# The down-projection of a gated unit turned round: output columns on the partitions, the gate kept in bf16 and transposed by DMA

## The chip, the cores and the metric

The kernel runs on one core of a Trainium2 chip. The metric is device time in microseconds. Before the change the median of three runs is 803.18 us (802.27 to 803.32). Short names: PE is TensorE, ACT is ScalarE, DVE is VectorE, POOL is GpSimd, SP is SyncE, which here only issues DMAs.

## The reference

Two sub-layers read the same normalised input, and one gates the other. S is 2048 tokens, D is 640, F is 1728, with 32 heads of 20 columns.

```python
x = A_x
xn = _layernorm(x, axis=-1)
s = _A_ref(xn, A_wqkv, A_wo)              # softmax attention, then @ wo
g = _silu(_B_ref(xn, B_w_gate, B_w_up, B_w_down))
return x + s * g
# _B_ref: h = sigmoid(x @ w_gate) * (x @ w_up); return h @ w_down
```

## The kernel before

**Stages.** A first stage, written out as a list of steps, normalises the tokens, transposes them into `xnT` (columns on the partitions, four chunks of 512 tokens) and makes the first keys, values and queries. Then comes one long stage in which everything else is interleaved, and a short tail for the last attention block and the last 512 tokens of the output.

**Attention.** Eight groups of four heads times four query chunks of 512 make 32 blocks. A score tile is 128 keys by 512 queries of one head. Its exponential is made either by ACT (two tiles at once, `pt`, or one, `px`) or by DVE with integer operations (`iv`, then three passes into `pb`, four tiles at once). PE adds the tiles times the values into `oacc`. After a block, DVE copies `oacc` to `on` (line 959), the row sums go to DRAM and back in another layout (`ld`, `lt`), DVE takes reciprocals (`rt`, line 969), these go to DRAM and come back spread out (`rd`, `rl`), and POOL multiplies (`on_bf`).

**The gated unit.** For each chunk c of 512 tokens there are 14 tiles kf of 128 hidden columns. `mk_gu` makes one of them: gate and up matmuls, tanh on ACT, and a multiply on DVE (line 690) that writes `hT[:, kf, :]`, with hidden columns on the partitions and tokens along the row. `mk_down(c, t4, h)` is the second matmul for 128 tokens (t4 of 4) and half of the output columns (h of 2, 320 columns). `hT` is the stationary operand and `wd` moves, 14 steps of four matmuls that lie side by side in the array (`cols`, line 471), each 32 columns of the stationary operand. ACT makes tanh (`td`), and DVE makes (td + 1) * ps in f32 (line 740), which is stored to `gq_dram` with tokens as rows (line 742). For the last chunk DVE writes it straight into SBUF (`gq_last`, line 736).

**The output.** `mk_out(tt, h)` multiplies the attention output by `wo` for token tile tt. `load_out(tt)` has loaded x (line 770) and the gate (line 771) into one of three buffers (tt modulo 3), and DVE multiplies the sum with the gate (line 795, `otmp`). POOL adds x, and the tile is stored. The last four token tiles are done in the tail (`t_main`, `t_rest`).

**What sets the order.** The orders of PE, ACT, DVE and POOL are written out at build time by a planner (the loop at line 1229). It steps a clock of its own with the durations of lines 444 to 448, and at each step gives a free engine its next instruction. PE chooses between score matmuls, value matmuls and an item (`Item`), which holds one of three shared PSUM banks from its first matmul until its last operation marked "free". A down item books 14 steps of 0.14 us on PE, 0.32 on ACT and 0.40 on DVE. Items of the gated unit come from `glu_items`, in order, as long as the work done is at most LEAD us ahead of what is due. M_ORD, DORD and XORD say in which order the three banks are tried for an item, for a DVE score tile and for an extra ACT score tile. The order on SP is not written out: the framework places DMAs by their own readiness, and SP works them in that order.

```python
    def cols(out, lhsT, rhs, start, stop):
        for j in range(0, P, 32):
            nc.tensor.matmul(out[j:j + 32, :], lhsT=lhsT[:, j:j + 32], rhs=rhs, start=start, stop=stop,
                             tile_position=(0, j), skip_group_check=True)
```

Of the kernel before, what the change touches and what calls it, by code (L numbers as in the profile page):

```python
# [18 lines left out]
P = 128  # L19
# [32 lines left out]
def kernel(  # L52
# [394 lines left out]
    LATE, T_LT, T_OU, T_L2, T_RL = 1.0, 9.0, 1.5, 4.5, 5.6  # L447
    T_PASS = (0.1333, 0.1333, 0.27)

    def t_exp(n):  # L450
# [213 lines left out]
    def mk_gu(c, kf, at):  # L664
# [18 lines left out]
            cols(st[key], w[:, i, kd, ko * P:ko * P + P], xnT[:, c, kd, :], kd == 0, kd == KD - 1)  # L683

        def th():
            st["t"] = w2.tile([P, QC], BF16, tag="tnh", bufs=2, name="tnh")
            act_imm(st["t"][0:fs, :], st["g"][0:fs, :], ACT.Tanh, 0.5)

        def ev():
# [4 lines left out]
            cols(st["g"], wgu_tiles[(c, k2)][:, 0, kd, P:2 * P], xnT[:, c, kd, :], kd == 0, kd == KD - 1)  # L694

        def th2():
            st["t"] = w2.tile([P, QC], BF16, tag="tnh", bufs=2, name="tnh")
            act_imm(st["t"][fs:P, :], st["g"][0:fs, :], ACT.Tanh, 0.5)

        def ev2():  # L700
# [9 lines left out]

    gq_l = []

    def gq_last(t4):
        if len(gq_l) == t4 // 2:
            w = w2.tile([P, 2, KD, 2 * P], BF16, tag="wgu", bufs=2, name="gql")
            gq_l.append(w.rearrange("p i k f -> p (i k f)").bitcast(FP32))
        return gq_l[t4 // 2][:, t4 % 2 * D:(t4 % 2 + 1) * D]

    def mk_down(c, t4, h, at):
        st = {}  # L720
        tt = 4 * c + t4
# [24 lines left out]


    FL, FG, FK = (NG - 1) * GC, (NG - 2) * GC, (KD - 1) * P
# [15 lines left out]
    def load_out(tt):  # L764
        if tt in out_tiles:
            return
        o2 = xfl[:, tt % 3 * KD * QC:tt % 3 * KD * QC + 3 * D]
        flush("o")
        out_tiles[tt] = (o2[:, 0:D], o2[:, D:3 * D].bitcast(FP32))
        nc.sync.dma_start(out=out_tiles[tt][0], in_=x2[tt * P:(tt + 1) * P, :])  # L770
        nc.sync.dma_start(out=out_tiles[tt][1], in_=gq_dram[tt * P:(tt + 1) * P, :])

    def mk_out(tt, h, at):
        st = {}

        def alloc():
            if h == 0:
                load_out(tt)
                if (tt + 1) % 4:
                    load_out(tt + 1)  # L780
            st["ps"] = misc_ps()

        def mm(kd):
            hs = slice(h * HD, (h + 1) * HD)
            cols(st["ps"][:, 0:HD], oU[:, kd, tt * P:(tt + 1) * P], wo[:, kd, hs], kd == 0, kd == KD - 1)

        def ev():
            xr, gqr = out_tiles[tt]
            sl = slice(h * HD, (h + 1) * HD)
            while sum(x[1] == "o" for x in pool_q) > 2:  # L790
                x = next(x for x in pool_q if x[1] == "o")
                pool_q.remove(x)
                x[2]()
            tmp = w2.tile([P, HD], FP32, tag="gqs", bufs=3, name="otmp")
            ins = nc.vector.scalar_tensor_tensor(out=tmp, in0=st["ps"][:, 0:HD], scalar=0.25,
                                                 in1=gqr[:, sl], op0=ALU.mult, op1=ALU.mult)
# [10 lines left out]
        return Item([("PE", alloc, [(0.136, lambda kd=kd: mm(kd)) for kd in range(KD)]),  # L807
                     ("DVE", 0.40, ev, "free", mark("o", tt, h))], at, need=ALT + 1 + 2 * (tt // 4),
                    pre=[("d", tt // 4, t4, i) for t4 in range(4) for i in range(2)] + [("h", 2, kf) for kf in range(NFT)] + (
                        [("o", tt - 2, 1)] if h == 0 and tt > 1 else []))  # L810


# [1 line left out]
    for c in range(NQC):  # L814
        for kf in range(NFT):
            glu.append(lambda at, c=c, kf=kf: mk_gu(c, kf, at))
        for h in range(2):
            for t4 in range(4):
                glu.append(lambda at, c=c, t4=t4, h=h: [mk_down(c, t4, h, at)])
# [273 lines left out]
    xg = xl.rearrange("p (t u) -> p t u", u=D)  # L1093

    def t_main(t4):
        nc.vector.scalar_tensor_tensor(out=tmps[t4], in0=mains[t4], scalar=0.25, in1=gq_last(t4)[:, 0:512],
                                       op0=ALU.mult, op1=ALU.mult)
        if t4 < 2:
            nc.gpsimd.tensor_tensor(out=tail[t4][:, 0:512], in0=tmps[t4], in1=tail[t4][:, 0:512], op=ALU.add)

    def t_rest(i):
        nc.vector.scalar_tensor_tensor(out=tmp[:, 2 * i:2 * i + 2, :],
                                       in0=rest[i][:, 0:2 * EX].rearrange("p (t e) -> p t e", e=EX),
                                       scalar=0.25, in1=gq_l[i].rearrange("p (t u) -> p t u", u=D)[:, :, 512:D],
                                       op0=ALU.mult, op1=ALU.mult)
        (nc.vector if i else nc.gpsimd).tensor_tensor(out=xg[:, 2 * i:2 * i + 2, 512:D], in0=tmp[:, 2 * i:2 * i + 2, :],
                                                      in1=xg[:, 2 * i:2 * i + 2, 512:D], op=ALU.add)
# [420 lines left out]
```

## Time and profile before

| | |
|---|---|
| median of three runs | 803.18 us |
| the profiled execution | 803.98 us |
| its span, first to last instruction | 802.3 us |
| granted TensorE clock | 1.00 |
| down matmuls (`bk<-wd,hT`, 320 columns) | 1792, mean 302 ns |
| gate and up matmuls (`bk<-xnT,wgu`, 512 columns) | 2160, mean 383 ns |
| tanh of a down item (`td`, 128x320) | 32, mean 617 ns |
| tanh of a gate item (`tnh`, 128x512) | 52, mean 790 ns |
| multiply of a down item (`gqs`, `gql`) | 32, median 480 to 482 ns |
| gate loads (`xnT<-gq_dram`, 320 KB) | 12 |
| gate stores (`gq_dram<-gqs`, 160 KB) | 24 |

A line of the timeline gives the start, the time from the first start to the last end of the merged instructions, the engine, the line of the kernel, the operation, and the tiles as output<-input. The duration of one instruction includes its way through the engine, and the next one starts before it ends, so the pace of an engine is read between starts. Line 82 is the helper that issues tanh and exp on ACT, and line 473 is the matmul in `cols`, for all items that use it; the tiles tell them apart. "SPq" is the time that SP takes to issue a DMA, not that of the transfer.

### The profile page before, as it was taken

The page shows a single profiled execution, that of the slowest core. Times are in us where ns is not written, and L with a number is a line of the kernel's source. Part 1 is how long each engine was busy: PE and PEld are TensorE (multiplying, and loading weights), DVE is VectorE, ACT ScalarE, POOL GpSimd, SP SyncE. Part 2 cuts the span into 40 slices and gives each one's busy share as a digit, 9 for nine tenths or more (in the row PEclk, how much of TensorE's full clock was granted, in tenths as well). Part 3 has the DMA queues.
Part 4 walks back from the last instruction along what each step waited for, and adds up shares of the span by engine and source line. Part 5 has one row for each costly group of instructions (what it writes and reads, how often), then busy time and mean ns, then how long its engine had stood idle before and what let it go on. Part 6 is the DMA issues. An engine that isn't in the chain of part 4 may idle for free.

```text
span 802.3 us, 25398 instructions
## 1 busy us (share of the span) xinstructions
PE 780.6 (97%) x10466; PEld 285.1 (36%) x10466; DVE 769.5 (96%) x1239; ACT 781.6 (97%) x991; POOL 106.2 (13%) x219
## 2 busy tenths in 40 slices
PE   8899999999999999999999999999999999999997
PEld 5523333333433323334332332333333233333333
DVE  7799999999999999989999999999999999999996
ACT  8799999999999999999999999999999999999994
POOL 7200000000000000000000010000000100502325
PEclk9999999999999999999999999999999999999999
DMA  5441212223122223222113133222311332330421
GB/s 162 133 130 49 69 40 75 63 66 81 47 63 66 73 72 100 52 57 71 49 47 94 53 86 76 76 79 58 98 37 61 91 89 53 106 103 23 141 62 62
DMA packets 91851, 60.47 MB, mean 75 GB/s; under 512 B 34891, under 2 KB 85627, under 8 KB 91735
## 3 DMA queue, kind: packets, MB, share of 16 engines
q1 hardware_dynamic: 91447, 58.52, 26.1%
q8 instruction: 82, 1.34, 0.7%
q14 instruction: 34, 0.28, 0.1%
q10 hardware_dynamic: 288, 0.33, 0.1%
HBM read 45.18 MB, written 11.09 MB: 70 GB/s over the span
## 4 chain that ended last, share of the span: by engine, by line
PE 48%; ACT 39%; DVE 6%; issue 5%; DMA 1%; SPq 0%; POOL 0%; DVEq 0%; ACTq 0%; POOLq 0%
ACT pt L82 31%; PE bk L473 20%; PE scA L889 15%; PE oacc L926 10%; ACT px L82 4%; ACT tnh L82 2%; DVE iv L1325 2%; DVE pb L1025 1%; PE bk L889 1%; ACT td L82 1%; PE tp L292 1%; DVE pb L1022 0%; DMA xt<-in_A_x_dram 0%; PE scrap L398 0%; PE psk L142 0%
## 5 line engine op out<-in xcount | busy, mean ns | idle before, releaser
L82 ACT ACTIVATE pt<-scA 128x1024 bf16<-128x1024 f32 (+1 forms) x709 | 708.8, 1189 | 1.0 <-PE scA L889 0.4
L1325 DVE TENSOR_SCALAR iv<-bk 128x512 int16<-128x512 f32 x500 | 332.9, 684 | 12.0 <-PE bk L889 9.6
L889 PE MATMUL scA<-q,kT 32*128 32x512 bf16 x1412 | 275.9, 382 | 8.7 <-ACT pt L82 3.3
L889 PE MATMUL bk<-q,kT 32*128 32x512 bf16 x636 | 207.4, 383 | 0.0
L889 PEld LDWEIGHTS <-kT 32*128 32x128 bf16 x2048 | 88.5, 91 | 262.0 <-issue 250.6
L926 PE MATMUL oacc<-pt,v 128*21 128x512 bf16 x1412 | 178.7, 381 | 0.7 <-ACT pt L82 0.7
L926 PE MATMUL oacc<-pb,v 128*21 128x512 bf16 x1000 | 161.4, 382 | 0.0
L473 PE MATMUL bk<-xnT,wgu 128*32 128x512 bf16 x2160 | 157.3, 383 | 0.5 <-DVE iv L1325 0.2
L1025 DVE TENSOR_TENSOR pb<-iv,pb 128x2048 bf16<-128x2048 bf16 x125 | 152.5, 1220 | 0.7
L979 POOL TENSOR_TENSOR on_bf<-on,rl 128x128 bf16<-128x128 f32 x116 | 54.4, 472 | 627.3 <-DVE iv L1325 170.4
L82 ACT ACTIVATE px<-bk 128x512 bf16<-128x512 f32 x136 | 101.4, 763 | 1.7 <-POOL hT L1167 1.6
L1019 DVE TENSOR_SCALAR pb<-iv 128x2048 int16<-128x2048 int16 x125 | 87.1, 697 | 0.4
L473 PE MATMUL bk<-wd,hT 128*32 128x320 bf16 x1792 | 87.0, 302 | 0.3 <-DVE iv L1325 0.2
L1022 DVE TENSOR_SCALAR pb<-iv 128x2048 int16<-128x2048 int16 x125 | 86.7, 693 | 0.0
L926 PEld LDWEIGHTS <-v 128*21 128x21 bf16 x2548 | 53.9, 91 | 76.0 <-issue 53.5
L473 PEld LDWEIGHTS <-wgu 128*32 128x32 bf16 x2160 | 44.4, 95 | 64.3 <-issue 45.9
L473 PEld LDWEIGHTS <-hT 128*32 128x32 bf16 x1792 | 37.5, 95 | 38.5 <-issue 32.9
L473 PE MATMUL bk<-xnT,wu 128*32 128x512 bf16 x640 | 48.5, 384 | 0.6 <-DVE iv L1325 0.2
L926 PE MATMUL oacc<-px,v 128*21 128x512 bf16 x136 | 46.7, 381 | 0.0
L82 ACT ACTIVATE tnh<-bk 128x512 bf16<-128x512 f32 (+1 forms) x56 | 43.4, 776 | 0.1
L690 DVE SCALAR_TENSOR_TENSOR hT<-tnh,bk 128x512 bf16<-128x512 bf16 x52 | 35.4, 681 | 1.0 <-PE bk L889 0.3
L800 POOL TENSOR_TENSOR xnT<-otmp,xnT 128x160 bf16<-128x160 f32 x48 | 28.2, 607 | 40.4 <-PE bk L889 15.9
(119 smaller groups left out, 413.6 us busy)
## 6 DMA issues: line engine op xcount, KB each, us to landing
rl<-rd SPq DMA_DIRECT2D x124, 64.0 KB
wgu<-in_B_w_gate_dram SPq DMA_DIRECT2D x24, 320.0 KB
wgu<-in_B_w_up_dram SPq DMA_DIRECT2D x24, 320.0 KB
gq_dram<-gqs SPq DMA_DIRECT2D x24, 160.0 KB
xnT<-gq_dram SPq DMA_DIRECT2D x12, 320.0 KB
xt<-in_A_x_dram SPq DMA_DIRECT2D x16, 160.0 KB
xnT<-in_A_x_dram SPq DMA_DIRECT2D x16, 160.0 KB
out_dram<-xnT SPq DMA_DIRECT2D x14, 160.0 KB
```

Of the source, the lines that this page charges most:

```text
L82: return nc.scalar.add_instruction(mybir.InstActivation(func=func, name=nc.get_next_instruction_name(), engine=ENG.Activation, ins=[nc.sca ...
L292: nc.tensor.transpose(out=tps[k][:, kd, :], in_=xns[k][:, kd * P:(kd + 1) * P], identity=ident)
L473: nc.tensor.matmul(out[j:j + 32, :], lhsT=lhsT[:, j:j + 32], rhs=rhs, start=start, stop=stop, tile_position=(0, j), skip_group_check=True)
L690: return nc.vector.scalar_tensor_tensor(out=hT[0:fs, kf, :], in0=st["t"][0:fs, :], scalar=1.0, in1=st["u"][0:fs, :], op0=ALU.add, op1=ALU. ...
L800: add = nc.gpsimd.tensor_tensor(out=xr[:, cs], in0=tmp[:, i * HD // 2:(i + 1) * HD // 2], in1=xr[:, cs], op=ALU.add)
L889: nc.tensor.matmul(dst, lhsT=kTs[gc_of(b)[0] % 2][32 * j:32 * j + 32, kt * P:(kt + 1) * P], rhs=qts[b % 3][32 * j:32 * j + 32, :], start=T ...
L926: nc.tensor.matmul(oacc[32 * j:32 * j + DH + 1, :], lhsT=lhsT, rhs=u["src"], start=first, stop=last, tile_position=(0, 32 * j), skip_group ...
L979: ins = nc.gpsimd.tensor_tensor(out=on_bf[:, cs], in0=on[:, cs], in1=rl[:, cs], op=ALU.mult)
L1019: ins = nc.vector.tensor_scalar(out=pb[:, 0, :, :].bitcast(I16), in0=iv, scalar1=0x7F80, scalar2=1, op0=ALU.bitwise_and, op1=ALU.bitwise_or)
L1022: ins = nc.vector.tensor_scalar(out=pb[:, 1, :, :].bitcast(I16), in0=iv, scalar1=0x007F, scalar2=0x3F00, op0=ALU.bitwise_and, op1=ALU.bitw ...
L1025: ins = nc.vector.tensor_tensor(out=pb[:, 1, :, :], in0=iv.bitcast(BF16), in1=pb[:, 1, :, :], op=ALU.mult)
L1325: beat(nc.vector.tensor_scalar(out=d["iv"][:, j, :], in0=bank[bk], scalar1=B_OFF, scalar2=0.0, op0=ALU.add, op1=ALU.max))
```

## The change

The down-projection swaps its operands. `wd` is stationary and `hT` moves, so that an item has 128 output columns on the partitions and all 512 tokens of the chunk along the row. There are five items for a chunk in place of eight, with 14 steps of four matmuls of 512 columns, a tanh of 512 and a multiply of 512, which now writes bf16. The gate is kept in DRAM as `gqT`, for each chunk 640 rows (columns of the output) of 512 tokens. `load_out` turns it with a transposing load of 640x128 into 128x640. In the last chunk each item's 128x512 result is copied from SBUF to SBUF by a transposing DMA, issued 1.5 us of the planner's clock after the multiply, and `gq_last` is one bf16 tile. The down items' tanh shares the buffers of the gate items' tanh (three in place of two and two). The output's product `otmp` is bf16 with buffers of its own. Four constants of the planner change too: LEAD 40 to 30, M_ORD 1 to 0, DORD 2 to 0, XORD 0 to 1.

```diff
-URGENT, ROUNDS, HOLD, SLACK, LEAD, LAG, D_LAST, D_LAST_END = 0.2, 6, 0.0, 0.0, 40.0, 2.0, 20, 20
-M_ORD, WAIT3, FALL, M_END = 1, 0.2, 1, 2.0
+URGENT, ROUNDS, HOLD, SLACK, LEAD, LAG, D_LAST, D_LAST_END = 0.2, 6, 0.0, 0.0, 30.0, 2.0, 20, 20
+M_ORD, WAIT3, FALL, M_END = 0, 0.2, 1, 2.0
-XMAX, DQ, DORD, XORD, STARVE = 2, 1.4, 2, 0, 0.3
+XMAX, DQ, DORD, XORD, STARVE = 2, 1.4, 0, 1, 0.3
...
-    gq_dram = dram.tile([S, D], FP32, name="gq_dram", tag="gqd", bufs=1)
+    gqT = dram.tile([NQC * D, QC], BF16, name="gqT", tag="gqd", bufs=1)
...
-    def mk_down(c, t4, h, at):
+    def mk_down(c, e, at):
...
         def mm(kf):
-            cols(st["ps"][:, 0:HD], hT[:, kf, t4 * P:(t4 + 1) * P], wd[:, kf, h * HD:(h + 1) * HD],
-                 kf == 0, kf == NFT - 1)
+            cols(st["ps"], wd[:, kf, e * P:(e + 1) * P], hT[:, kf, :], kf == 0, kf == NFT - 1)
 
         def th():
-            st["td"] = w2.tile([P, HD], BF16, tag="td", bufs=2, name="td")
-            act_imm(st["td"], st["ps"][:, 0:HD], ACT.Tanh, 0.25)
+            st["td"] = w2.tile([P, QC], BF16, tag="tnh", bufs=3, name="td")
+            act_imm(st["td"], st["ps"], ACT.Tanh, 0.25)
 
         def ev():
-            if c == NQC - 1:
-                return nc.vector.scalar_tensor_tensor(out=gq_last(t4)[:, h * HD:(h + 1) * HD], in0=st["td"], scalar=1.0,
-                                                      in1=st["ps"][:, 0:HD], op0=ALU.add, op1=ALU.mult)
-            flush("o")
-            gqs = w2.tile([P, HD], FP32, tag="gqs", bufs=3, name="gqs")
-            ins = nc.vector.scalar_tensor_tensor(out=gqs, in0=st["td"], scalar=1.0, in1=st["ps"][:, 0:HD],
+            gqs = w2.tile([P, QC], BF16, tag="gqs", bufs=2, name="gqs")
+            ins = nc.vector.scalar_tensor_tensor(out=gqs, in0=st["td"], scalar=1.0, in1=st["ps"],
                                                  op0=ALU.add, op1=ALU.mult)
-            nc.sync.dma_start(out=gq_dram[tt * P:(tt + 1) * P, h * HD:(h + 1) * HD], in_=gqs)
+            if c < NQC - 1:
+                nc.sync.dma_start(out=gqT[c * D + e * P:c * D + (e + 1) * P, :], in_=gqs)
+            else:
+                timed.append((now + T_GT, lambda: nc.sync.dma_start_transpose(
+                    out=gq_last()[:, :, e * P:(e + 1) * P], in_=gqs)))
             return ins
-        return Item([("PE", alloc, [(0.14, lambda kf=kf: mm(kf)) for kf in range(NFT)]),
-                     ("ACT", 0.32, th), ("DVE", 0.40, ev, "free", mark("d", c, t4, h))], at, pre=[("h", c, kf) for kf in range(NFT)])
+        return Item([("PE", alloc, [(T_MM, lambda kf=kf: mm(kf)) for kf in range(NFT)]),
+                     ("ACT", 0.48, th), ("DVE", 0.60, ev, "free", mark("d", c, e))], at, pre=[("h", c, kf) for kf in range(NFT)])
...
-        nc.sync.dma_start(out=out_tiles[tt][1], in_=gq_dram[tt * P:(tt + 1) * P, :])
+        nc.sync.dma_start_transpose(out=out_tiles[tt][1], in_=gqT[c * D:(c + 1) * D, t4 * P:(t4 + 1) * P])
...
-            tmp = w2.tile([P, HD], FP32, tag="gqs", bufs=3, name="otmp")
+            tmp = w2.tile([P, HD], BF16, tag="ot", bufs=3, name="otmp")
```

More of the change, by code (lines that the diff above doesn't have):

```diff
@@ L446 @@
     T_IV, T_ON = 0.605, 0.60
-    LATE, T_LT, T_OU, T_L2, T_RL = 1.0, 9.0, 1.5, 4.5, 5.6
+    LATE, T_LT, T_OU, T_L2, T_RL, T_GT = 1.0, 9.0, 1.5, 4.5, 5.6, 1.5
     T_PASS = (0.1333, 0.1333, 0.27)
@@ L685, in th @@
         def th():
-            st["t"] = w2.tile([P, QC], BF16, tag="tnh", bufs=2, name="tnh")
+            st["t"] = w2.tile([P, QC], BF16, tag="tnh", bufs=3, name="tnh")
             act_imm(st["t"][0:fs, :], st["g"][0:fs, :], ACT.Tanh, 0.5)
@@ L696, in th2 @@
         def th2():
-            st["t"] = w2.tile([P, QC], BF16, tag="tnh", bufs=2, name="tnh")
+            st["t"] = w2.tile([P, QC], BF16, tag="tnh", bufs=3, name="tnh")
             act_imm(st["t"][fs:P, :], st["g"][0:fs, :], ACT.Tanh, 0.5)
@@ L711, with gq_last @@
     gq_l = []
-    def gq_last(t4):
-        if len(gq_l) == t4 // 2:
+    def gq_last():
+        if not gq_l:
             w = w2.tile([P, 2, KD, 2 * P], BF16, tag="wgu", bufs=2, name="gql")
-            gq_l.append(w.rearrange("p i k f -> p (i k f)").bitcast(FP32))
-        return gq_l[t4 // 2][:, t4 % 2 * D:(t4 % 2 + 1) * D]
-    def mk_down(c, t4, h, at):
+            gq_l.append(w.rearrange("p i k f -> p (i k f)")[:, 0:4 * D].rearrange("p (t u) -> p t u", u=D))
+        return gq_l[0]
+    def mk_down(c, e, at):
         st = {}
-        tt = 4 * c + t4
         def alloc():
@@ L766, in load_out @@
             return
-        o2 = xfl[:, tt % 3 * KD * QC:tt % 3 * KD * QC + 3 * D]
+        c, t4 = divmod(tt, 4)
+        o2 = xfl[:, tt % 3 * KD * QC:tt % 3 * KD * QC + 2 * D]
         flush("o")
-        out_tiles[tt] = (o2[:, 0:D], o2[:, D:3 * D].bitcast(FP32))
+        out_tiles[tt] = (o2[:, 0:D], o2[:, D:2 * D])
         nc.sync.dma_start(out=out_tiles[tt][0], in_=x2[tt * P:(tt + 1) * P, :])
-        nc.sync.dma_start(out=out_tiles[tt][1], in_=gq_dram[tt * P:(tt + 1) * P, :])
+        nc.sync.dma_start_transpose(out=out_tiles[tt][1], in_=gqT[c * D:(c + 1) * D, t4 * P:(t4 + 1) * P])
     def mk_out(tt, h, at):
@@ L808, in mk_out @@
                      ("DVE", 0.40, ev, "free", mark("o", tt, h))], at, need=ALT + 1 + 2 * (tt // 4),
-                    pre=[("d", tt // 4, t4, i) for t4 in range(4) for i in range(2)] + [("h", 2, kf) for kf in range(NFT)] + (
+                    pre=[("d", tt // 4, i) for i in range(KD)] + [("h", 2, kf) for kf in range(NFT)] + (
                         [("o", tt - 2, 1)] if h == 0 and tt > 1 else []))
@@ L816 @@
             glu.append(lambda at, c=c, kf=kf: mk_gu(c, kf, at))
-        for h in range(2):
-            for t4 in range(4):
-                glu.append(lambda at, c=c, t4=t4, h=h: [mk_down(c, t4, h, at)])
+        for e in range(KD):
+            glu.append(lambda at, c=c, e=e: [mk_down(c, e, at)])
     for t in range(4 * NVP):
@@ L1095, in t_main @@
     def t_main(t4):
-        nc.vector.scalar_tensor_tensor(out=tmps[t4], in0=mains[t4], scalar=0.25, in1=gq_last(t4)[:, 0:512],
+        nc.vector.scalar_tensor_tensor(out=tmps[t4], in0=mains[t4], scalar=0.25, in1=gq_last()[:, t4, 0:512],
                                        op0=ALU.mult, op1=ALU.mult)
@@ L1103, in t_rest @@
                                        in0=rest[i][:, 0:2 * EX].rearrange("p (t e) -> p t e", e=EX),
-                                       scalar=0.25, in1=gq_l[i].rearrange("p (t u) -> p t u", u=D)[:, :, 512:D],
+                                       scalar=0.25, in1=gq_last()[:, 2 * i:2 * i + 2, 512:D],
                                        op0=ALU.mult, op1=ALU.mult)
```

## Prediction

> **What bounds the kernel now.** I read the busy times first, then the chain of work that ended last, then the table of busy time by stretches, and last the timeline of a down-projection stretch and of the output stretch.
>
> ```profile
> PE 780.6 (97%) x10466; PEld 285.1 (36%) x10466; DVE 769.5 (96%) x1239; ACT 781.6 (97%) x991; POOL 106.2 (13%) x219
> ...
> PE 48%; ACT 39%; DVE 6%; issue 5%; DMA 1%; SPq 0%; POOL 0%; DVEq 0%; ACTq 0%; POOLq 0%
> ACT pt L82 31%; PE bk L473 20%; PE scA L889 15%; PE oacc L926 10%; ACT px L82 4%; ACT tnh L82 2%; DVE iv L1325 2%; DVE pb L1025 1%; PE bk L889 1%; ACT td L82 1%; PE tp L292 1%; DVE pb L1022 0%; DMA xt<-in_A_x_dram 0%; PE scrap L398 0%; PE psk L142 0%
> ```
>
> No single engine is the bound: PE, ACT and DVE are each busy 96 to 97% of the span, and the chain hops between PE and ACT. The stretches show where the rest is lost (columns: busy time of PE, PEld, DVE, ACT, POOL):
>
> ```profile
> 20.00:60.00 40.00, 37.58 (x448) 16.91 (x450) 34.45 (x61) 35.78 (x51) 4.10 (x8) 1.00 0.46 132
> 60.00:100.00 40.00, 39.82 (x509) 12.10 (x501) 37.92 (x59) 40.00 (x50) 1.83 (x4) 1.00 0.22 58
> ...
> 200.00:240.00 40.00, 39.46 (x621) 15.22 (x617) 38.84 (x64) 40.00 (x53) 3.61 (x8) 1.00 0.19 54
> ```
>
> From 60 us on ACT has no idle time to speak of, and where down items run (200 to 240) DVE lacks 1.2 of 40 us. Granted clock is 1.00 throughout. So a saving counts only as far as it takes work off a saturated engine, and the issue order is fixed at build time: it cannot rearrange itself around a late transfer.
>
> **The matmuls of the down-projection.** Before there are 32 items of 14 groups, each group four matmuls of 320 columns side by side: 448 groups. After there are 20 items of 14 groups of 512 columns: 280. The pace is read between starts, since a matmul's own time (302 and 383 ns) holds its pipeline:
>
> ```profile
> 210.15 1.41 PE L473 MATMUL bk<-wd,hT 128*32 128x320 bf16 x36
> ...
> 211.49 0.39 PE L889 MATMUL scA<-q,kT 32*128 32x512 bf16 x2
> ...
> 211.81 0.73 PE L473 MATMUL bk<-wd,hT 128*32 128x320 bf16 x16
> ...
> 212.47 0.39 PE L889 MATMUL scA<-q,kT 32*128 32x512 bf16 x2
> ```
>
> Nine groups and one change to score matmuls take 211.49 - 210.15 = 1.34 us, four take 0.66, so a group takes 0.68 / 5 = 0.136 us. The same reading of the 512-column gate matmuls (16 matmuls 678.90 to 679.88, 8 from 680.19 to 680.74) gives 0.215. So 448 x 0.136 = 60.9 becomes 280 x 0.215 = 60.2: 0.7 us less, although there are 672 fewer matmuls. The planner books 62.7 and 59.7, so its clock gains 3.0 where the engine gains 0.7. Of PE's work in the helper of line 473 (762 groups of 512 columns, 448 and 120 of 320, together 241 us by these paces) the chain holds 20% of 802.3 = 160 us, two thirds; I count 0.67 x 0.7 = **0.5 us**.
>
> **Tanh and multiply.** The pace of a 320-column tanh is 203.58 - 203.27 = 0.31 us (start of td to start of the next exp), of a 512-column one 678.45 - 677.97 = 0.48. 32 x 0.31 = 9.9 becomes 20 x 0.48 = 9.6: 0.3 less, of which the chain's 0.7% (5.6 us of td) makes half, **0.2 us**. On DVE, gqs to the next start takes 0.39 to 0.40 us and the 512-column multiply of line 690 takes 0.59 (702.47 to 703.06): 32 x 0.395 = 12.6 becomes 11.8. The 0.8 us is off the chain, but score tiles can be given to either engine: a tile costs ACT 0.45 us (a 1024-wide exp each 0.91) and DVE 0.60 + 2.34 / 4 = 1.19, so a microsecond of DVE is worth 0.45 / (0.45 + 1.19) = 0.28 us if the planner uses it: **0.2 us**. Both ends: nothing, and 0.8.
>
> **PSUM banks.** An item holds one of three shared banks until its multiply is done. That tail was 1.2 us from td's start to the end of the multiply (209.00 to 210.24). Twelve fewer tails free 14 us, and 20 tails longer by 0.36 take back 7. Seven bank-microseconds of 2400 are worth nothing that I can read; DVE's iv waited for PE 9.6 us in all, and a 0.3% share of that is nothing. I take 0.
>
> **Stores, loads, copies.** Twenty-four stores of 160 KB become 15 of 128 KB, each one SP issue of 0.35 us; no engine waited for them but POOL, which is 13% busy. Twelve plain loads of the gate become 12 transposing loads of half the bytes, and five transposing copies are new on SP. No transposing transfer is in this trace, so I bound it by its rows. Landing: the chain has one plain load at 3.21 us from issue. The lower end is that time; the upper is five times, 16 us, if 640 short row pieces in place of 128 long ones set it. Holding SP: from 0.36 us (the plain issue) to 1.8 (five such issues, one for each 128 columns); a copy 0.36 to 1.4. What is late first is read here:
>
> ```profile
> 690.13 1.24 SPq L771 DMA_DIRECT2D xnT<-gq_dram  x2
> ...
> 749.74 0.56 SPq L961 DMA_DIRECT2D ld<-on  x1
> 750.40 0.39 SPq L771 DMA_DIRECT2D xnT<-gq_dram  x1
> 751.69 0.33 SPq L963 DMA_DIRECT2D lt<-ld  x1
> ```
>
> ```profile
> 697.24 0.48 DVE L795 SCALAR_TENSOR_TENSOR otmp<-bk,xnT 128x320 f32<-128x320 f32 x1
> ...
> 753.83 0.25 DVE L969 RECIPROCAL rt<-lt 128x16 f32<-128x16 f32 x1 [0.41 <-DMA lt<-ld]
> ```
>
> By the three buffers, the load at 690.13 is that of token tile 3 (its buffer came free when tile 0's second multiply ended at 688.0); its first use is at 697.24, 7.1 us later, and the other late ones have 10 us or more (740.72 for 750.81, 773.89 for 786.36). A landing of twice 3.2 us is still in time. On SP the gap between ld and lt is the 2 us that ld takes to land, and a load held up to 1.3 us fits into it. I take **0**, the row it is nearest to by bytes, and keep the rest as a rival. In the last chunk the gate now goes through a copy, but the last down item ends at 771.3 and its first use is at 794.3: 23 us of cover.
>
> The Trainium skill, VectorE: DVE Perf Modes, section "The three transpose paths", gives 1309 ns for a 128x128 transpose by DMA; five in a row would make an estimated 6.5 us a load, which still meets the 7.1 us. Its Advanced Engine Details and Errata, section "X-Bar Transpose (TRN2)", says transposing DMAs are as fast as plain ones. No run here shows either yet; by both the sum stays the same, and only the rival's chance moves.
>
> **Output and tail.** The 24 output multiplies and 6 of the tail read a bf16 gate in place of f32, with the other operand in PSUM: gqs with a bf16 operand took 482 ns, otmp with f32 478, so 0. POOL's adds read bf16: at most a little less, off the chain.
>
> **Planner constants.** LEAD 40 to 30 lets gate and up items run ahead 10 us of PE work less. They fill PE from 45 to 140 us (484 matmuls, 121 groups, 26 us), with PE at 39.84 of 40 between 40 and 80 us, where DVE is idle 3.1 us (busy 9.02 of 10, 9.90 of 10, 18.00 of 20). Less of that work gives those score fills back: between 0 and 3.1 x 0.28 = 0.9 us; I take **0.7**, near the upper end, since PE is what DVE lacks there. The other three constants change which bank is tried first. No row prices that; an order can gain no more than ACT's idle time from 20 to 780 us (760 - 754.9 = 5 us), and I put the same 5 us on the other side. I take 0.
>
> **Sum.** -0.5 - 0.2 - 0.2 - 0.7 = -1.6. The profiled execution took 803.98 us (span 802.3 and 1.7 around it), 0.8 above the median of 803.18; the terms are differences, so I take them off the median: 803.2 - 1.6 = **801.6**, and since every term came from whole durations I round it to 801.5, own range 799 to 803.
>
> **Rivals.** (1) *SP held and loads late, slower.* Between 686 and 708 and between 740 and 756 SP is nearly always issuing. If a transposing transfer holds it 1.8 us, each of the three late norms (ld at 749.7 and 771.0, and the one at 704.5) is late by up to 1.5 us, its reciprocal holds DVE and all score work queued behind it, and PE waits for the bank: the 0.41 us wait above shows that no slack is left. Three times 1.5 is 4.5, less the 0.9 of engine work saved: 803.2 + 3.6 = 806.8. It decides from 1.3 us of hold, or from a landing over 7.1 us; at 16 us tile 3 alone is 9 late and the sum is near 820. For it: the static order. Against: three buffers and 7 us of lead. (2) *Gain lost*: ACT sets the end and the constants give nothing: 803.2 - 0.4 = 802.8. For it: ACT idle of 0 from 60 us. (3) *The new order is better or worse by itself*: 798 or 806.5, by most of the 5 us. (4) *The transposes fall apart into single elements*: 82,000 pieces a load, at 0.26 x 802 x 16 / 91,447 = 0.037 us of one engine each, is 190 us a load, far over 1,000 us. Nothing speaks for it but that the trace has no such transfer.
>
> **How the numbers follow.** Forecast 0.45 (0.30 beyond the bound, 0.15 within); late transfers 0.19; gain lost 0.13 (within); better order 0.10 and worse order 0.12; single elements 0.01. About 0.2%, 1.6 us, is what a measurement can tell from no change. So faster 0.40, same 0.28, slower 0.32. The range takes both orders and the first price of the late transfers: 797.5 to 808.
>
> **What would show it.** 1120 wd matmuls at a 0.215 us pace; 20 tanh and multiplies of 512 columns; DVE idle between 40 and 80 us under 3 us; reciprocals waiting no more than 1.7 us for lt, output multiplies none for their load. It is wrong if SP's transposing issues last over 1.3 us each, if waits for lt or for the gate grow, or if ACT shows new idle time in mid-kernel.

## The result, and the profile after

The changed kernel takes 808.08 us (median of six runs, 805.86 to 808.87), the kernel before on the same chip 803.15 (six runs, 802.27 to 804.27): ratio 1.0057, interval 1.0046 to 1.0067, slower by 4.6 us. The forecast was 801.5. The profiled execution of the changed kernel took 805.86 us (span 804.1) and is the shortest of its six. It shows 1.8 us of the loss; four of the others have spans of 806.1 to 807.2 and a mean granted clock of 0.992 in place of 0.999, which is taken up below.

The engines did what was expected. First the busy times of the page, then groups by tile (busy time, mean ns | idle before them), both of the changed kernel:

```profile
PE 775.5 (96%) x9794; PEld 264.3 (33%) x9794; DVE 769.2 (96%) x1227; ACT 781.6 (97%) x983; POOL 107.2 (13%) x219
...
L473 PE MATMUL bk<-hT,wd 128*32 128x512 bf16 x1120 | 82.6, 383 | 2.6 <-DVE iv L1323 2.3
```

```profile
L82 ACT ACTIVATE td<-bk 128x512 bf16<-128x512 f32 x20 | 14.5, 725 | 0.0
...
L967 DVE RECIPROCAL rt<-lt 128x16 f32<-128x16 f32 x31 | 7.6, 246 | 3.7 <-DMA lt<-ld 3.7
```

There are 1120 matmuls and 20 tanhs, as forecast. But before the down matmuls there is an idle time of 2.6 us, and the reciprocals wait 3.7 us for `lt`; before the change that was 1.7 us, also in two waits. The table of stretches tells where the time went (columns: busy time of PE, PEld, DVE, ACT, POOL, then the granted clock). Before, then after:

```profile
640.00:680.00 40.00, 39.87 (x541) 12.71 (x533) 39.53 (x59) 40.00 (x52) 3.66 (x8) 1.00 0.28 72
720.00:760.00 40.00, 39.48 (x623) 15.09 (x625) 38.31 (x64) 39.62 (x50) 12.59 (x24) 1.00 0.26 75
```

```profile
60.00:100.00 40.00, 39.34 (x514) 11.78 (x506) 39.55 (x61) 40.00 (x52) 1.81 (x4) 1.00 0.23 59
...
640.00:680.00 40.00, 39.45 (x509) 12.66 (x511) 37.01 (x57) 39.94 (x51) 3.65 (x8) 1.00 0.22 57
720.00:760.00 40.00, 36.54 (x515) 12.17 (x513) 36.86 (x59) 38.11 (x48) 8.74 (x17) 1.00 0.24 52
```

From 60 to 100 us DVE is now busy 39.55 in place of 37.92: the smaller LEAD does fill the early gap. DVE then idles 3.0 us from 640 to 680, where it idled 0.5. From 720 to 760 all three engines lose together: PE 2.9 us, DVE 1.5, ACT 1.5. Most of that is one stall, at block 28's normalisation. SP's issues there, before and then after (start, duration):

```profile
723.91 2.76 SPq L1009 DMA_DIRECT2D oU<-on_bf  x3
726.78 0.53 SPq L961 DMA_DIRECT2D ld<-on  x1
...
728.48 0.36 SPq L963 DMA_DIRECT2D lt<-ld  x1
```

```profile
725.54 0.76 SPq L1007 DMA_DIRECT2D oU<-on_bf  x1
726.41 1.25 SPq L739 DMA_TRANSPOSE gql<-gqs  x1
727.71 0.75 SPq L1007 DMA_DIRECT2D oU<-on_bf  x1
728.56 0.53 SPq L959 DMA_DIRECT2D ld<-on  x1
729.14 1.51 SPq L1007 DMA_DIRECT2D oU<-on_bf  x2
730.75 0.42 SPq L961 DMA_DIRECT2D lt<-ld  x1
```

And what follows on DVE and PE, before and then after (in brackets the idle time before, and what ended it):

```profile
730.05 0.25 DVE L969 RECIPROCAL rt<-lt 128x16 f32<-128x16 f32 x1 [1.28 <-DMA lt<-ld]
```

```profile
732.37 0.25 DVE L967 RECIPROCAL rt<-lt 128x16 f32<-128x16 f32 x1 [2.58 <-DMA lt<-ld]
...
735.08 1.26 PE L473 MATMUL bk<-hT,wd 128*32 128x512 bf16 x20 [2.08 <-DVE iv L1323]
```

The copy of the sums, `on`, starts at 724.25 (before: 723.31). `ld` is issued 4.3 us later (before 3.5): the first store ahead of it in SP's queue starts 1.3 us after the copy (before 0.6), and a transposing copy of 1.25 us stands there besides two stores (before three stores). Two more stores stand between `ld` and `lt` (before one), so the reciprocal finds its sums 1.3 us later still than before (wait 2.58 against 1.28). DVE has the reciprocal next in its order and waits; PE waits for the banks that DVE empties. A second wait, of 1.16 us, follows at block 30. There a transposing load stands between `ld` and `lt`, and `lt` leaves 2.8 us after `ld` (before 1.7):

```profile
771.55 0.56 SPq L959 DMA_DIRECT2D ld<-on  x1
773.14 1.14 SPq L770 DMA_TRANSPOSE xnT<-gqT  x1
774.38 0.53 SPq L961 DMA_DIRECT2D lt<-ld  x1
```

```profile
777.40 0.25 DVE L967 RECIPROCAL rt<-lt 128x16 f32<-128x16 f32 x1 [1.16 <-DMA lt<-ld]
```

### The profile page after: what moved, and what is told of

It is laid out like the page before. It is cut to its first block, busy times and chain, and to the rows that moved or that the text cites. A ratio compares the mean times of both kernels' runs of the same rounds, so it can differ in the third digit from the quotient of the medians.

```text
span 804.1 us, 24023 instructions
## 1 busy us (share of the span) xinstructions
PE 775.5 (96%) x9794; PEld 264.3 (33%) x9794; DVE 769.2 (96%) x1227; ACT 781.6 (97%) x983; POOL 107.2 (13%) x219
## 3 DMA queue, kind: packets, MB, share of 16 engines
q8 instruction: 76, 1.25, 0.6%
## 5 line engine op out<-in xcount | busy, mean ns | idle before, releaser
L82 ACT ACTIVATE pt<-scA 128x1024 bf16<-128x1024 f32 x707 | 698.6, 1164 | 3.3 <-PE bk L887 2.7
L887 PE MATMUL bk<-q,kT 32*128 32x512 bf16 x642 | 204.1, 383 | 1.1 <-DVE otmp L794 0.6
L924 PE MATMUL oacc<-pt,v 128*21 128x512 bf16 x1406 | 185.2, 382 | 0.9 <-ACT pt L82 0.8
L887 PEld LDWEIGHTS <-kT 32*128 32x128 bf16 x2048 | 85.5, 91 | 287.5 <-issue 277.4
L473 PE MATMUL bk<-xnT,wgu 128*32 128x512 bf16 x2160 | 159.2, 383 | 0.8
L473 PE MATMUL bk<-hT,wd 128*32 128x512 bf16 x1120 | 82.6, 383 | 2.6 <-DVE iv L1323 2.3
L924 PE MATMUL oacc<-px,v 128*21 128x512 bf16 x142 | 48.6, 382 | 0.0
L82 ACT ACTIVATE tnh<-bk 128x512 bf16<-128x512 f32 (+1 forms) x56 | 41.7, 745 | 0.1
L799 POOL TENSOR_TENSOR xnT<-otmp,xnT 128x160 bf16<-128x160 bf16 x48 | 29.6, 637 | 46.0 <-DVE pb L1020 26.8
L473 PEld LDWEIGHTS <-wd 128*32 128x32 bf16 x1120 | 20.6, 95 | 35.5 <-issue 29.2
```

What stands on the lines that cost most here:

```text
L82: return nc.scalar.add_instruction(mybir.InstActivation(func=func, name=nc.get_next_instruction_name(), engine=ENG.Activation, ins=[nc.sca ...
L887: nc.tensor.matmul(dst, lhsT=kTs[gc_of(b)[0] % 2][32 * j:32 * j + 32, kt * P:(kt + 1) * P], rhs=qts[b % 3][32 * j:32 * j + 32, :], start=T ...
L924: nc.tensor.matmul(oacc[32 * j:32 * j + DH + 1, :], lhsT=lhsT, rhs=u["src"], start=first, stop=last, tile_position=(0, 32 * j), skip_group ...
```

## The experiments

All times are medians; the ratio is to the kernel before, run on the same chip beside the experiment (803.4 to 803.8 us).

**The changed kernel again.** Nothing edited.

> The changed kernel once more, unaltered, beside the others of this call. All theories: 806 to 809. Theory A2 (late norms: the reciprocal on DVE waits for lt, because ld and lt stand behind other DMAs in SP's one queue; the waits stop all engines, and the stop lets the granted clock of PE drop for a few us more): in a profile with clock 0.992 the drop lies right behind a wait of rt, and the span is 2 to 3 us longer than with 0.999. Rival C: the drop lies elsewhere.

807.46 us (806.69 to 808.04), 1.0051 (1.0037 to 1.0066). This profile has a span of 805.4 and shows what the first one lacked: the same gap (2.11 us before the down matmuls at 734.69), and then the granted clock (third column from the end, after the busy times):

```profile
734.00:736.00 2.00, 1.31 (x23) 0.57 (x22) 1.97 (x5) 0.46 (x1) 0.00 (x0) 1.00 0.27 95
736.00:738.00 2.00, 2.00 (x18) 0.35 (x19) 1.81 (x3) 1.02 (x1) 0.00 (x0) 0.50 0.60 105
738.00:740.00 2.00, 2.00 (x21) 0.29 (x17) 1.15 (x2) 1.46 (x2) 0.00 (x0) 0.65 0.03 4
740.00:742.00 2.00, 2.00 (x34) 0.69 (x34) 2.00 (x3) 2.00 (x4) 0.46 (x1) 1.00 0.00 0
```

TensorE runs at half clock from 736.0 to 739.4 and does half the work there (18 and 21 matmuls in 2 us against 34). So a gap of 2 us costs itself and, in some executions, up to another 1.7 (half of the 3.4 us).

**Plain transfers.** The 17 transposing DMAs become plain ones of the same bytes, in the same places of the queue; the gate is then not transposed.

```diff
-                timed.append((now + T_GT, lambda: nc.sync.dma_start_transpose(
-                    out=gq_last()[:, :, e * P:(e + 1) * P], in_=gqs)))
+                timed.append((now + T_GT, lambda: nc.sync.dma_start(
+                    out=gq_last()[:, :, e * P:(e + 1) * P], in_=gqs.rearrange("p (t q) -> p t q", q=P))))
...
-        nc.sync.dma_start_transpose(out=out_tiles[tt][1], in_=gqT[c * D:(c + 1) * D, t4 * P:(t4 + 1) * P])
+        nc.sync.dma_start(out=out_tiles[tt][1].rearrange("p (e q) -> p e q", q=P), in_=gqT[c * D:(c + 1) * D, t4 * P:(t4 + 1) * P].rearrange("(e p) q -> p e q", p=P))
```

> The changed kernel with its 12 transposing loads and 5 transposing copies made plain DMAs of the same bytes and pieces; every engine and SP keep the same order. It leaves the gate's 128x128 blocks unturned. Theory A (a transposing DMA holds SP 1.2 us where a plain one holds 0.35, so the DMAs of the norms behind it come late, the reciprocal on DVE waits for lt and all engines stand): SP's issues fall to about 0.4 us, the longest wait of rt for lt falls from 2.6 to under 1.5 us, PE's 2.1 us gap near 734 us goes, and the span falls by 1 to 2 us, the median from 808 to 803 to 805. Rival B (the new issue order by the planner's constants and the longer items costs the time): within 1 us of 808. Rival C (the clock drop seen in four of six runs of the changed kernel has nothing to do with the gap): clock 0.992 as often as before.

805.4 us (804.31 to 806.46), 1.0021 (1.0012 to 1.0030): about 2.7 us of the loss goes (from 1.0054, the mean of the changed kernel's two measurements). Yet the wait at block 28 is still there:

```profile
731.68 0.26 DVE L967 RECIPROCAL rt<-lt 128x16 f32<-128x16 f32 x1 [2.39 <-DMA lt<-ld]
```

So the transposing transfers alone are not the cause: with plain ones `ld` leaves 3.8 us after the copy in place of 4.3, and the wait falls by 0.2 us only. What went is the wait at 777. It was 1.2 us; how the rest of the 2.7 us comes about, the traces do not say. The stores that wait for POOL hold the queue too.

**Old constants, and new constants alone.** The changed kernel with the four planner constants of before (the diff), and the kernel before with the four new ones (the same turned round).

```diff
-URGENT, ROUNDS, HOLD, SLACK, LEAD, LAG, D_LAST, D_LAST_END = 0.2, 6, 0.0, 0.0, 30.0, 2.0, 20, 20
-M_ORD, WAIT3, FALL, M_END = 0, 0.2, 1, 2.0
+URGENT, ROUNDS, HOLD, SLACK, LEAD, LAG, D_LAST, D_LAST_END = 0.2, 6, 0.0, 0.0, 40.0, 2.0, 20, 20
+M_ORD, WAIT3, FALL, M_END = 1, 0.2, 1, 2.0
...
-XMAX, DQ, DORD, XORD, STARVE = 2, 1.4, 0, 1, 0.3
+XMAX, DQ, DORD, XORD, STARVE = 2, 1.4, 2, 0, 0.3
```

> The changed kernel with the four planner constants of the kernel before (LEAD 40, M_ORD 1, DORD 2, XORD 0). Theory A: the late norms fall elsewhere against the transposing DMAs, so the waits of rt for lt move but do not vanish: 804 to 809. Rival B: the loss is the constants', 802 to 804.

> The kernel before with the four constants of the changed one. Theory A: the constants alone are worth little, 801 to 804.5, and rt waits for lt no more than 2 us in all. Rival B: 806 to 809, with new gaps on PE or ACT in mid-kernel.

808.52 us, 1.0053 (1.0040 to 1.0066), and 811.03, 1.0100 (1.0084 to 1.0115). Each half alone makes the kernel slower, by 0.5% and 1.0%, and both together by 0.57%: the two don't add up. For the constants alone 801 to 804.5 was expected, and 806 to 809 by the rival; both were too low. In each kernel the profile shows long waits at late norms: waits for `lt` of 2.1 and 2.4 us in the first, of 1.9, 3.6 and 0.7 in the second, with a spell of half clock behind the two of the first and the 3.6 of the second.

**The sums' wait taken away.** The reciprocal of blocks 27 to 30 reads a tile of ones in place of `lt`, so that these blocks are not normalised; every instruction and every transfer stays, in the same order. Done to the changed kernel, to the kernel before, and to that with the new constants.

```diff
-        beat(nc.vector.reciprocal(out=rt, in_=lt), False)
+        beat(nc.vector.reciprocal(out=rt, in_=lt if b < NBLK - 5 else lt0), False)
```

> The changed kernel with the reciprocals of the last four norms (blocks 27 to 30) read from a constant tile in place of lt; ld and lt are still transferred, the orders of all engines and of SP stay. It leaves those blocks unnormalised. Theory A2: no waits of rt, no PE gap at 734 us, clock 0.997 or more, and the median falls by 4 to 6 us to 802 to 804. Rival B (order and longer items): falls by under 1.5 us.

> The same edit in the kernel before (reciprocals of the last four norms from a constant tile, so those blocks stay unnormalised). Theory A2: it has only 1.7 us of such waits to lose and no clock drop behind them, so it falls by 1 to 2 us, to 801.5 to 802.8, and stands within 1.5 us of the changed kernel with the same edit. Rival B: no change, and the changed kernel with the edit still 3 us or more behind.

> The kernel before with the changed kernel's four constants and the same edit (last four norms unnormalised). With the constants alone it was at 811.0 with 6.2 us of rt waits. Theory A2: it falls to 802 to 805. Rival B: the constants' order is slow by itself, and it stays above 807.

Changed: 805.21, 1.0017 (1.0008 to 1.0026). Before: 802.98, 0.9996 (0.9987 to 1.0005). Before with the new constants: 804.94, 1.0020 (1.0011 to 1.0029), down from 1.0100. The same edit is worth nothing in the old kernel, 0.34% (2.7 us) in the changed one and 0.8% (6.4 us) in the one with new constants. In the changed kernel 4 to 6 us were expected, and it was expected to come within 1.5 us of the kernel before with the same edit; it stays 1.7 us behind. Its profile shows the second half of the same chain:

```profile
759.71 1.27 POOL L982 TENSOR_TENSOR on_bf<-on,rl 128x512 bf16<-128x512 f32 x1 [2.66 <-DMA rl<-rd]
...
761.45 0.49 DVE L794 SCALAR_TENSOR_TENSOR otmp<-bk,xnT 128x320 bf16<-128x320 f32 x1 [1.84 <-POOL xnT L799]
```

POOL's product waits for the broadcast sums `rl`, the adds of the output stand behind it on POOL, and DVE's output multiply waits for those adds to free its buffer.

**Both waits taken away.** POOL's product of blocks 29 and 30 reads `on` twice in place of `rl`, besides the edit above; in the changed kernel and in the one before. The order of the engines stays; on SP one load moves back in each kernel, a gate load in the changed one and an x load in the one before.

```diff
-            nc.gpsimd.tensor_tensor(out=on_bf, in0=on, in1=rl, op=ALU.mult)
+            nc.gpsimd.tensor_tensor(out=on_bf, in0=on, in1=on, op=ALU.mult)
```

> The changed kernel with both waits on the late norms' round trips taken away: the reciprocals of the last four norms read a constant tile, and POOL's product of the last two reads on twice in place of rl (two attention blocks come out wrong, two more unnormalised); all transfers stay, one load of the gate moves behind four stores on SP. Theory A3 (what the change itself does to the engines is a small gain, as forecast, and all of the loss comes from SP's one queue: first by rt's waits, then by POOL waiting for rl with the output's adds behind it, on which otmp waits 1.8 us): 801 to 803. Rival D (the rest of the loss is the longer items or the order): stays at 804.5 to 805.5.

> The same two edits in the kernel before, with the same parts wrong. Theory A3: little left to win, 802 to 803.2, at or just above the changed kernel with these edits. Rival D: 802 to 803.2, two or more below it.

Changed 801.88, 0.9978 (0.9969 to 0.9987); before 802.28, 0.9983 (0.9975 to 0.9992). The late norms' waits thus cost the changed kernel 1.0054 - 0.9978 (the mean of its two measurements, and this) = 0.0076, 6.1 us, and the kernel before 0.0017, 1.4 us. The difference, 4.7 us, is the whole loss; without the waits the change is worth 0.4 us, with an uncertainty of about 1.

**Plain transfers without the sums' wait.**

> The changed kernel with plain transfers in place of the 17 transposing ones (gate blocks unturned) and the last four norms' reciprocals from a constant tile. Plain transfers alone gave a ratio to before of 1.0021, the constant tile alone 1.0017. Theory A3: the hold of SP by transposes hurts through the same waits, among them POOL's for rl, so the two together give 1.000 or less (801.5 to 803.5). Rival E (transposes cost something else, on the memory ports): the two gains add up in full, to 0.998 or less. Rival D: no better than 1.0015.

805.09, 1.0013 (1.0003 to 1.0023), against 1.0017 with transposing ones: once the reciprocal doesn't wait, it makes no measurable difference whether the transfers transpose, to within about 1 us. So the expectation (1.000 or less) fails: plain transfers do not shorten what is left, and POOL still waits 6.3 us for `rl` (6.0 with transposing ones).

**The reciprocal later.** Two ways, both complete kernels. First block 28's alone at the 9 us that earlier blocks have:

```diff
-                    timed.append((free["DVE"] + (T_LT if norm_pending[0] < NBLK - 4 else T_L2), norm_pending[0]) + norm_a(norm_pending[0]))
+                    timed.append((free["DVE"] + (T_LT if norm_pending[0] < NBLK - 3 else T_L2), norm_pending[0]) + norm_a(norm_pending[0]))
```

> The changed kernel with one norm's reciprocals booked 9.0 us after the copy of oacc as for all earlier blocks, in place of 4.5 (block 28, whose wait for lt is the longest, 2.6 us; its result is needed only with block 29). SP's transposing DMAs stay. Theory A: the 2.6 us wait and PE's gap of 2.1 us go, the clock stays at 0.999 or more in nearly all runs, and the median falls by 2 to 5 us to 803 to 806. Rival B: within 1.5 us of 808. Rival C: the gap goes and the clock is still 0.992 in most runs.

809.59, 1.0072 (1.0059 to 1.0084), and the expectation fails: the order after it shifts, and the stall moves to block 29, where `ld` now stands behind four stores of 3.73 us and more:

```profile
757.11 0.25 DVE L967 RECIPROCAL rt<-lt 128x16 f32<-128x16 f32 x1 [6.29 <-DMA lt<-ld]
```

Then the booked time of all late reciprocals, T_L2, from 4.5 to 6.5 us: in the changed kernel, in the one before, in the one before with the new constants, and in the changed one with the old constants; and 7.5 in the changed one.

```diff
-    LATE, T_LT, T_OU, T_L2, T_RL, T_GT = 1.0, 9.0, 1.5, 4.5, 5.6, 1.5
+    LATE, T_LT, T_OU, T_L2, T_RL, T_GT = 1.0, 9.0, 1.5, 6.5, 5.6, 1.5
```

> The changed kernel, complete, with the reciprocals of the last three norms booked 6.5 us after the copy of oacc in place of 4.5 (T_L2), near the time at which lt lands in the trace (5.6 to 8.1 us after the copy's end). Theory A3: rt waits fall from 3.7 us to under 1.5 and the clock drop behind them goes: 803 to 806; the end may come up to 1 us later. A risk that both theories share: SP's order moves and another norm is hit, as when only block 28 was booked later (809.6).

> The kernel before, complete, with one planner constant changed (T_L2, the booked time from the store ld to the reciprocal of blocks 27 to 30, 4.5 to 6.5 us), as it was in the changed kernel at 802.25 us (0.9984). Theory (the change itself is worth about -1.6 us, and its loss was the reciprocal that came too early for its sums): the kernel before loses little from its waits for lt (1.7 us in all), so the later reciprocal gives it at most that: 802 to 803.5 us, ratio 0.998 to 1.0005, and stays above the changed kernel with the same constant. Rival (the later reciprocal is worth about as much in any of these orders, so that the gain was not the change's): 801.5 to 802.2, no slower than the changed kernel with it.

> The kernel before with the four new planner constants and T_L2 6.5. With 4.5 it took 811.0 us, and 804.9 with the reciprocals freed from their sums. Theory (the new constants alone cost the old items nearly nothing once the sums are in time): the waits for lt fall below 1 us each, and the time to 803 to 805.5, ratio 1.000 to 1.0025. Rival (the constants themselves make an order that stalls elsewhere): 807 or more, with waits over 1.5 us on DVE left after 700 us.

> The changed kernel, complete, with the four old planner constants and T_L2 6.5: the transposed items and transfers alone, with the sums in time. With 4.5 it took 808.5 us. Theory (items -0.9 us by the forecast's terms, LEAD -0.7 missing): 802 to 803.5, ratio 0.998 to 1.000. Rival (the gain of the changed kernel at 6.5 comes from the new constants, and the transposed items bring nothing): 803.5 to 805.

> The changed kernel, complete, with T_L2 7.5 in place of 4.5, one more than the 6.5 that took 802.25 us. Theory (at 6.5 only waits of 0.9 and 0.2 us for lt are left): these go, at most 1 us better: 801.3 to 802.5, ratio 0.997 to 0.999. Rival (a later reciprocal makes rl and with it POOL's product late, so that the output product waits for POOL instead): 803 to 806, with a wait over 1 us before otmp or on POOL for rl.

| kernel | T_L2 4.5 | T_L2 6.5 |
|---|---|---|
| before | 1 | 803.12, 0.9996 (0.9987 to 1.0005) |
| before, new constants | 1.0100 | 808.47, 1.0067 (1.0055 to 1.0079) |
| changed, old constants | 1.0053 | 803.18, 0.9996 (0.9987 to 1.0004) |
| changed | 1.0057, 1.0051 | 802.25, 0.9984 (0.9975 to 0.9993) |

The changed kernel with 6.5 is the best complete one: 802.25 us, 1.3 below the kernel before, an interval that leaves out 1 by little. The waits for `lt` fall from 3.7 to 1.0 us in all. The later reciprocal gives the old kernel nothing, so the gain isn't one that any order has. It's no rule either, and two expectations fail here: with the new constants alone, where 803 to 805.5 was expected, the wait stays (2.46 us at 758.84), and with 7.5 the changed kernel is at 807.59, 1.0050 (1.0037 to 1.0063), where 801.3 to 802.5 was expected. In the profile of that one, the longest of its six executions (809.72), the reciprocal of block 29 waits 1.84 us, PE stops 2.10 us, and the clock is at half from 759.3 to 779.8.

**The transfers on another queue.** In the changed kernel, complete and with T_L2 4.5, first `ld` and `lt` of blocks 27 to 30 are issued by POOL (the first pair of the diff, and `ld` in the same way), then in their place the stores `oU<-on_bf` of blocks 26 to 28 (the second pair).

```diff
-        nc.sync.dma_start(out=lt, in_=ld.rearrange("j (i c) -> (j i) c", c=GH * QC // P))
+        (nc.sync if b < NBLK - 5 else nc.gpsimd).dma_start(out=lt, in_=ld.rearrange("j (i c) -> (j i) c", c=GH * QC // P))
...
-                timed.append((now + T_OU * i, lambda o=o, x=x: nc.sync.dma_start(out=o, in_=x)))
+                timed.append((now + T_OU * i, lambda o=o, x=x: (nc.sync if b < NBLK - 6 else nc.gpsimd).dma_start(out=o, in_=x)))
```

> The changed kernel, complete, all constants as they are (T_L2 4.5): only the two transfers of the row sums, ld and lt, of blocks 27 to 30 are issued from POOL in place of SP. Theory (the sums come late because ld and lt stand in SP's queue behind stores that wait for POOL and behind the transposing transfers): both waits for lt (2.6 and 1.2 us in the changed kernel) fall under 1 us, and the time to 803 to 806 us, ratio 0.9995 to 1.003, with what then waits for rl left. Rival (the two transfers themselves take longer than the 4.5 us, whichever queue issues them, or POOL is held by its own products): the waits stay at 2 us or more, and the time at 806.5 or above.

> The changed kernel, complete, all constants as they are: the stores oU<-on_bf of blocks 26 to 28, which wait for POOL's product at the head of SP's queue, are issued from POOL behind that product; ld and lt stay on SP. Theory in its narrow form (the stores that wait for POOL are the head of the queue that holds ld for over 2 us at 726): the wait of 2.6 us at 732 falls under 1 us; the wait at 777 (1.2 us, behind transposing copies) stays; 803.5 to 806.5 us. Rival (the transposing transfers of 1.2 us each are enough to hold ld): the wait at 732 stays over 1.5 us, and the time at 806 or above.

In the waits both theories hold, in the time neither. With the sums on POOL's queue the two waits fall from 2.6 and 1.2 us to 0.2 and 0.7, though the transfers are the same; with only the stores gone from SP, the wait at block 28 falls to 0.57 and the later one stays (2.06). That places the cause of these two waits in what stands ahead of `ld` and `lt` on SP; at block 28 it is the stores above all. But the times are 811.3, 1.0093 (1.0077 to 1.0108), and 807.1, 1.0038 (1.0024 to 1.0051). The first kernel's chain goes on like this:

```profile
756.35 1.15 SPq L770 DMA_TRANSPOSE xnT<-gqT  x1
757.59 0.53 SPq L969 DMA_DIRECT2D rd<-rt  x1
...
759.45 1.72 SPq L972 DMA_DIRECT2D rl<-rd  x4
```

```profile
763.16 1.26 POOL L982 TENSOR_TENSOR on_bf<-on,rl 128x512 bf16<-128x512 f32 x1 [4.51 <-DMA rl<-rd]
```

```profile
764.89 0.49 DVE L794 SCALAR_TENSOR_TENSOR otmp<-bk,xnT 128x320 bf16<-128x320 f32 x1 [4.17 <-POOL xnT L799]
```

Block 29's reciprocal starts at 753.93 and waits for nothing, but its result leaves SP only at 757.59, behind an x load that waits for its buffer and a transposing load. `rl` is late, POOL waits 4.51 us, DVE 4.17, PE 3.41, and half clock for 6.8 us follows. Taking one transfer out of the queue uncovers the next one in it.

## Why the prediction was wrong

The step that failed is the term **"Stores, loads, copies"**, taken at 0 because a load held up to 1.3 us "fits" into SP's gap. In its place the runs show waits at the late norms behind SP's queue that cost 4.7 us more than before (6.1 against 1.4). Not all of the 4.7 is the new transfers' own: where the stores stand in the queue also goes by the planner's order, another term taken at 0. Point by point:

- *Matmuls, tanh, multiply*: right in size. After the change a tanh starts 0.48 us before the next exp (204.73 to 205.21), the multiply takes 0.59 (206.37 to 206.96), and runs of two and of three groups of down matmuls (0.62 and 0.83 us) differ by 0.21 us, the paces that were used. Their sum of -0.9 was not seen by itself: without the late waits the whole change is worth -0.4 us, give or take 1.
- *LEAD, -0.7*: its sign in the profile came (DVE idle from 40 to 80 us falls from 3.1 to 1.5), its gain didn't. DVE had as many score tiles to do as before (500 `iv` in both), and the time it won early it idled away later, 3.0 us between 640 and 680. At block 27's `on` copy the changed kernel is not ahead (705.28 against 703.06, though its profile starts no slower). The kernel before with the four constants alone shows the same (DVE idle 1.4 us from 40 to 80 and 2.6 from 640 to 680), so the idle time moved with the constants. The factor of 0.28 assumed that the planner gives DVE more tiles; it gave none.
- *SP's hold, 0.36 to 1.8 us, "up to 1.3 us fits"*: the hold was 1.14 to 1.28 us, inside what was thought harmless. The failure is the gap that was looked at. The 2 us between `ld` and `lt` was checked for one more issue. At block 28 the delay arises ahead of `ld`, where the queue holds stores that wait for POOL, and these and the copy add up: of the 1.3 us by which the wait grew, 1.1 stay with plain transfers. At block 30 a load of 1.14 us did come between `ld` and `lt`, but late in the gap, and `lt` left 2.8 us after `ld` in place of 1.7. The row with 0.41 us of wait, and the 1.28 us at 730.05, which the prediction does not show, said that the reciprocal had no slack: any delay of SP there had a price from the first tenth on, not from 1.3 us.
- *Landing*: right in the main. No output multiply waits for a gate load in the profile after, and in the repeat one waits 0.3 us.
- *Rival 1* named the mechanism, at a chance of 0.19, but not the place: its three norms are those of blocks 27, 29 and 30 (`ld` at 704.5, 749.7 and 771.0), and it leaves out block 28 (726.78), where the longest wait stands, before as after. That its time comes near (806.8 against 808.1) is partly luck, since it took a delay of 1.5 us at each of the three. In fact two norms wait, block 28's 1.3 us longer than before and block 30's 1.2 us, while block 29's wait of 0.4 goes. The waits for `rl` cost as much again (0.0039, 3.1 us, between the two experiments that differ in them alone), and half clock follows some of the gaps. No term priced either of the two.
- *Rival 3* (the order by itself, up to 5 us either way) is hard to hold apart from rival 1: constants alone lose 8 us, and they change no transfer. The long waits that were followed up are late norms behind SP's queue, and edits of the order, wanted or not, move the time by up to 1%. But the 0.24% by which the new constants stay behind once the reciprocals do not wait (1.0020 against 0.9996) was not traced, so a cost of the order itself is not excluded.

What stays open: the exact share of half clock in the median. A mean clock of 0.992 against 0.999 would be some three such spells of 3.4 us (each lowers the mean by 1.7 / 806 = 0.002), but those executions left no trace. One of the three may lie at the start: 16 of the 20 traces have a spell that begins between 8 and 31 us, the first profiles of both kernels have none. How the 0.4 us that is left splits into items and constants is below what these runs tell.

## What to carry to other kernels

Where a short transfer feeds a wait that already shows in the profile, everything ahead of it in its in-order queue has a price, the waiting stores as well as the new issues: add them up to the first waiting transfer, and not only in the gap that looks free. When an order is fixed at build time by booked durations, give the booked wait its measured length after the change (one number was worth 5.6 us here, 1.0054 to 0.9984), and expect that any edit reshuffles such waits, so measure each variant and take no single one as the change's worth. Price a gap of TensorE above its own length (here 1.7 us more for each 3.4 us at half clock, where it follows).

## What the runs showed of the hardware

**Half clock after short gaps.** Every spell of half clock between 700 and 790 us in the traces lasts a multiple of 3.4 us, and a PE gap goes ahead of each (in the longest gap it starts within it). Whether a gap is followed by one, and how long it lasts, does not go by the gap's length:

| kernel | PE gap, us | half clock, us |
|---|---|---|
| changed, old constants | 0.99 | 3.4 |
| stores on POOL's queue, at 779 | 1.06 | none |
| plain transfers, no wait for sums | 1.31 | 6.8 |
| changed, old constants, T_L2 6.5 | 1.32 | none |
| changed, no wait for sums | 1.35 | 3.4 |
| before, new constants, at 716 | 1.43 | none |
| before, new constants, T_L2 6.5 | 1.67 | 6.8 |
| stores on POOL's queue, at 762 | 1.69 | 6.8 |
| changed, old constants | 1.77 | 3.4 |
| plain transfers | 1.89 | none |
| changed, first profile | 2.08 | none |
| changed, T_L2 7.5 | 2.10 | 20.5 |
| changed, repeat | 2.11 | 3.4 |
| before, new constants, at 757 | 3.07 | 3.4 |
| sums on POOL's queue | 3.41 | 6.8 |
| late reciprocal of block 28 | 5.21 | 6.8 |

Here are two rows of the kernel with the stores on POOL's queue, in which PE is idle for most of the first stretch and at half clock in the second:

```profile
762.00:764.00 2.00, 0.37 (x5) 0.07 (x8) 0.91 (x2) 1.64 (x3) 2.00 (x5) 1.00 0.05 13
...
766.00:768.00 2.00, 2.00 (x16) 0.42 (x19) 2.00 (x4) 1.62 (x3) 0.66 (x2) 0.50 0.36 117
```

The kernel before (T_L2 4.5 and 6.5) and the changed one at 6.5, with no gap over 1.0 us there, have no such spell. The Trainium skill, TensorE: Matmul & The Clock Gate, section "Part 1: The HAM clock gate (the "warmup" mystery)", describes free-running windows of about 3.4 us after which the clock is set to half or full; the lengths here agree. The Trainium skill's section "HAM oscillation — how this bites in real kernels" on the same page gives the rule "no PE-idle gaps >~3.4µs"; here gaps of 0.99 to 2.11 us were followed by half clock, and the measurement decides. That the same gap of 2.1 us led to it in one execution and not in another would fit windows that don't start with the kernel; no run here shows the windows themselves.

**A transposing DMA holds SP's queue.** Its issue takes 1.17 us where it loads 640x128 from DRAM and 1.24 us where it copies 128x512 within SBUF; in the run with plain transfers the same places take 0.38 and 0.68 us. The rows of the changed kernel give the least, middle and longest in ns:

```profile
L770 SPq DMA_TRANSPOSE xnT<-gqT x12: 1137/1168/1255, 537.0 to 773.1; - x12
```

```profile
L739 SPq DMA_TRANSPOSE gql<-gqs x5: 1213/1235/1278, 692.3 to 746.2; - x5
```
